# Attention with nine consecutive tokens of a head in a partition, K^T V in 64-row products, and its scaling on ScalarE

## The chip, the cores and the metric

One NeuronCore of a Trainium2 chip runs the whole program. The metric is the device time of one execution in microseconds (us); lower is better. TensorE multiplies, VectorE, ScalarE and GpSimd do elementwise work, reductions and copies, SP issues most of the transfers (DMAs). In the profile they are PE (PEld for its weight loads), DVE, ACT, POOL and SP.

## The reference

The inputs are float32; q, k and v are [8, 8, 576, 64]: batch, head, token, head dimension. What matters here is the first of three stages:

```python
q_s = exp(q - max(q, axis=-1)); q_s /= sum(q_s, axis=-1) + 1e-9     # over the 64 dims of a token
k_s = exp(k - max(k, axis=2));  k_s /= sum(k_s, axis=2) + 1e-9      # over the 576 tokens of a head
kv  = einsum('bhsd,bhse->bhde', k_s, v)                             # 64 x 64 for each head
out = einsum('bhsd,bhde->bhse', q_s, kv)
```

The output, 4608 tokens of 512, goes through a layer with eight experts (each token to its best one) and then through a gated layer, (x wa) * (x wb) wo.

## The kernel before

The attention works on 16 units, each of four heads of one batch: unit u is batch u // 2, heads 4(u % 2) to 4(u % 2) + 3. `load` (L79) puts 512 of a head's 576 tokens on 128 partitions, four consecutive tokens to a partition; the last 64 tokens of two batches share one extra tile (`s`), a batch on each half of the partitions, loaded with the unit of the even batch. So each step of a unit has a part for the 512 tokens and one for the 64, the latter often only in units of an even batch (`first`, L105).

- K: `kmax` (L118) reduces each partition's four tokens on VectorE; `kmax_t` turns the result (and the 64 extra tokens) by TensorE transposes (L100); `kmax_r` (L136, L139, L141) reduces over partitions and joins both parts; `kb_t` and `kb_c` (L152) bring the maximum back to all partitions; `ksub` (L161, L164) subtracts on GpSimd; `kexp` (L170, L171) takes the exponential on ScalarE; `vcopy` (L178, L180) copies V beside a column of ones.
- `kv_mm` (L217) forms K^T V for two heads at a time, with the sum of the exponentials in the ones' column: four products with 128 rows and one with 64 for each pair of heads, all into one PSUM tile. A float32 product is two records in the trace, a transpose one. `kv_norm` (L225, L226, L230) adds 1e-9, takes the reciprocal and scales the 64x64 diagonal blocks into `kvb`, all on VectorE. `kv_t`, `kv_c` (L240), `kv_g` (L246) and `kv_gc` (L249) multiply `kvb` with the gate weights and append the result.
- Q: `qmax` (L187, L191), `qsub` (L200, L206), transposes (`q_t`, `qs_t`) and exponentials on the way out of PSUM (`q_e` L260, `qs_e` L271).
- Output: `o_m` (L306) multiplies Q with `kvb`; `evac_l` (L276) copies the logits on ScalarE, then `evac_x` (L284 to L286) scales the rows on VectorE. Both read one PSUM tile, and the VectorE part waits for the ScalarE part. `out_shared` (L330) does this for the 64 extra tokens of two batches, 64 columns to each half of the PSUM partitions.
- After every second batch `route` (L337) chooses the experts on VectorE, stores x (L390) and the extra rows (L395) to DRAM, and builds one-hot matrices (L397) that ScalarE scales (L401, L402).

The order on each engine is the order of the program, and it is written out by hand. Step s runs this list, a name and how many units it is behind (`more` lets the routing go on, `shared` is `out_shared`):

```python
STEP = (("kv_t", 2), ("kmax_t", 0), ("kv_c", 2), ("q_t0", 1), ("kmax_r", 0), ("kv_g", 2), ("more", 2),
        ("kv_gc", 2), ("qmax", 0), ("q_e0", 1), ("kb_t", 0), ("kb_c", 0), ("qs_t", 1), ("ksub", 0), ("q_t1", 1),
        ("more", 2), ("o_m0", 2), ("qs_e", 1), ("q_e1", 1), ("kv_mm", 1), ("kmax", -1), ("vcopy", 0),
        ("o_m2", 2), ("o_l0", 2), ("more", 3), ("more", 3), ("more", 4), ("o_x0", 2), ("qsub", 0), ("kexp", 0),
        ("kv_norm", 1), ("o_l2", 2), ("o_x2", 2), ("shared", 2))
```

`run` (L433) issues the loads of K three units ahead and of Q and V two ahead, on SP. From step 10 on, the weights of the first expert are loaded and split, and later its first tokens are gathered and multiplied, between these operations; a table of places in the list (`AT`, L418) says where. Transposes share three PSUM tiles (`pt`), `kv_mm` has one (`pk`), the outputs two. The input buffers lie in memory that the expert stage uses later (`Experts.buffers`, L907).

## Time and profile before

| | us |
|---|---|
| median of three runs | 1457.78 (1457.41 to 1458.32) |
| the profiled execution | 1467.53 |
| its span in the trace | 1465.8 |
| busy in the span: PE, DVE, ACT, POOL | 1366.1, 1043.0, 674.0, 564.2 |

The profile comes from one execution. Times are counted from the start of its span, and L is a line of the kernel. An instruction's idle time is that of its engine just before it; behind the arrow stands what ended it.

### The profile page before, as it was taken

To read this page: it belongs to the slowest core of one execution; us is meant where nothing else is said; L and a number is where in the kernel's file an instruction comes from. 1 tells how busy PE (TensorE), PEld (TensorE's weight loads), DVE (VectorE), ACT (ScalarE), POOL (GpSimd) and SP (SyncE) were. 2 spreads that over 40 slices of the span, in tenths; PEclk is the share of its full clock that TensorE was granted. 3 is DMA by queue.
4 is the path that set the end of the run, shared out by engine and by line. 5 is a ranking of instruction groups with operands and counts; after the bars stand their busy time and mean duration, and the time that the engine had idled before them with its cause. 6 is when DMAs were issued, how large, how long until landed. Compare 5 with 4: busy or idle time off the path is not lost.

```text
span 1465.8 us, 29137 instructions
## 1 busy us (share of the span) xinstructions
PE 1366.1 (93%) x11068; PEld 1112.0 (76%) x11068; DVE 1043.0 (71%) x2340; ACT 674.0 (46%) x1625; POOL 564.2 (38%) x698
## 2 busy tenths in 40 slices
PE   6887898998999999989999999999999999999996
PEld 4776775665576676768888888888888888888885
DVE  5889875875687776426767867777777777767764
ACT  4556554753455454324444444444444444444432
POOL 6755521523334354104343343433334333343433
PEclk9988798999999999999999999999999999999998
DMA  9998245788564345126010010100101001010000
GB/s 240 253 251 220 73 131 164 268 291 271 184 220 140 113 135 165 48 72 255 2 56 4 1 59 1 59 1 16 45 1 59 2 18 42 1 59 1 31 1 30
DMA packets 87919, 145.87 MB, mean 100 GB/s; under 512 B 19792, under 2 KB 60752, under 8 KB 85584
## 3 DMA queue, kind: packets, MB, share of 16 engines
q1 hardware_dynamic: 81136, 123.85, 26.8%
q0 software_dynamic: 6080, 19.95, 4.2%
q8 instruction: 92, 1.51, 0.5%
q14 instruction: 67, 0.55, 0.1%
q10 hardware_dynamic: 544, 0.02, 0.0%
HBM read 149.78 MB, written 46.44 MB: 134 GB/s over the span
## 4 chain that ended last, share of the span: by engine, by line
PE 41%; DVE 10%; issue 2%; ACT 1%; POOL 1%; POOLq 0%; DVEq 0%; ACTq 0%
PE ab L1644 27%; PE mp L1659 13%; DVE raw L1348 1%; DVE y L1338 1%; DVE gp L1686 1%; DVE w L1348 1%; PE ab L1328 1%; DVE ysb L1818 1%; DVE w L1819 1%; DVE xg L1806 1%; DVE g L1819 1%; DVE gu L1815 0%; DVE w L1822 0%; DVE g L1822 0%; DVE y L1736 0%
## 5 line engine op out<-in xcount | busy, mean ns | idle before, releaser
L1644 PEld LDWEIGHTS <-gw 128*128 128x128 f16 x3780 | 369.2, 98 | 60.0 <-issue 13.6
L1644 PE MATMUL ab<-raw,gw 128*128 128x256 f16 x2100 | 280.2, 272 | 5.6 <-ACTq L1267 2.7
L1644 PE MATMUL ab<-w,gw 128*128 128x256 f16 x1680 | 225.2, 273 | 0.8
L1659 PEld LDWEIGHTS <-gp 128*128 128x128 f16 x1944 | 190.8, 98 | 25.9 <-ACT gp L1681 2.1
L1061 PEld LDWEIGHTS <-w 128*128 128x128 f16 x1824 | 180.1, 99 | 38.6 <-issue 12.7
L1061 PE MATMUL ph<-xhl,w 128*128 128x256 f16 x1728 | 198.2, 276 | 9.7 <-issue 4.1
L1078 PE MATMUL py<-w,hh 128*128 128x512 f16 x576 | 172.5, 381 | 2.4 <-DMA w<-wd 2.4
L1659 PE MATMUL mp<-wo,gp 128*128 128x256 f16 x756 | 142.6, 273 | 0.0
L1686 DVE SCALAR_TENSOR_TENSOR gp<-gp,gs 128x256 f16<-128x256 f16 x162 | 81.1, 505 | 59.0 <-ACT gp L1681 58.0
L1069 DVE SCALAR_TENSOR_TENSOR hl<-ph,hh 128x256 f16<-128x256 f32 x144 | 59.2, 420 | 78.7 <-ACT hh L1068 75.6
L1078 PE MATMUL py<-w,hl 128*128 128x512 f16 x288 | 109.9, 382 | 0.0
L1078 PEld LDWEIGHTS <-hh 128*128 128x128 f16 x608 | 59.8, 99 | 64.7 <-issue 4.2
L1460 POOL TENSOR_TENSOR gf<-gf 128x256 f32<-128x256 f32 x72 | 64.5, 916 | 100.4 <-ACT gf L1503 92.0
L1681 ACT ACTIVATE gp<-g 128x256 f16<-128x256 f32 x108 | 45.0, 417 | 115.7 <-DVE g L1822 114.8
L1644 PEld LDWEIGHTS <-w 128*128 128x128 f16 x756 | 73.7, 97 | 29.5 <-issue 21.0
L1717 POOL TENSOR_TENSOR gs<-w 128x256 f32<-128x256 f32 x54 | 39.5, 732 | 134.0 <-DVE w L1822 134.0
L1681 ACT ACTIVATE gp<-w 128x256 f16<-128x256 f32 x54 | 22.5, 417 | 148.9 <-DVE w L1822 146.2
L1659 PE MATMUL mp<-raw,gp 128*128 128x256 f16 x324 | 88.6, 273 | 0.9 <-DVE gp L1686 0.9
L1659 PE MATMUL mp<-w,gp 128*128 128x256 f16 x324 | 88.8, 274 | 0.0
L1068 ACT ACTIVATE hh<-ph 128x256 f16<-128x256 f32 x144 | 54.0, 378 | 74.9 <-PE ph L1061 74.5
L1023 POOL DMA_INDIRECT xg<-xd,gidx x40 | 43.9, 1098 | 106.9 <-ACT xhl L1052 51.4
L1815 DVE TENSOR_TENSOR gu<-tables,ab 128x256 f32<-128x256 f32 x108 | 45.3, 419 | 54.2 <-PE ab L1644 47.1
(337 smaller groups left out, 2798.8 us busy)
## 6 DMA issues: line engine op xcount, KB each, us to landing
w<-wd SPq DMA_DIRECT2D x58, 1024.0 KB
raw<-in_moe_w_dram SPq DMA_DIRECT2D x24, 512.0 KB
yd<-ysb SPq DMA_DIRECT2D x19, 513.0 KB
xd<-x SPq DMA_DIRECT2D x8, 1026.0 KB
y<-yd SPq DMA_DIRECT2D x8, 1026.0 KB
w<-in_k_dram SPq DMA_DIRECT2D x16, 512.0 KB
wd<-wst SPq DMA_DIRECT2D x16, 512.0 KB
g<-in_moe_w_a_dram SPq DMA_DIRECT2D x12, 512.0 KB
```

The source lines that it names most:

```text
L1023: nc.gpsimd.indirect_dma_start(out=self.x[:, j], out_offset=None, in_=self.xd[0:4 * S if s == 0 else NTOK, :], in_offset=bass.IndirectOffs ...
L1061: nc.tensor.matmul(ph, self.w1[:, w, k, o], x[:, k], start=i == 0, stop=i == 11)
L1068: nc.scalar.activation(self.hh[:, f], ph, AF.Relu)
L1069: nc.vector.scalar_tensor_tensor(self.hl[:, f], ph, 0.0, self.hh[:, f], ALU.max, ALU.subtract)
L1078: nc.tensor.matmul(self.py[j], h[:, f, o], self.w2[:, w, f], start=f == 0 and i == 0, stop=f == 7 and i == 2)
L1460: self.nc.gpsimd.tensor_tensor(s[:, dst], s[:, x], s[:, y], ALU.subtract)
L1644: self.nc.tensor.matmul(ps, self.w[f][:, b, o:o + P], self.y[n].op[:, a, yl, 256 * k:256 * k + 256], start=i == 0 and fresh, stop=i == 5, ...
L1659: self.nc.tensor.matmul(self.acc[nm][:, t], x, y, start=i == t == j == 0 and nm != "p3", stop=i == last and t == 1 and j == 2, skip_group_ ...
L1681: self.nc.scalar.activation(self.part(i, a)[:, 0], x, AF.Copy, scale=2.0 ** -11)
L1686: eng.scalar_tensor_tensor(p[:, 1], p[:, 0], -2048.0, x, ALU.mult, ALU.add)
L1717: pool.tensor_tensor(x, a11, a21, ALU.subtract)
L1815: v.tensor_tensor(u, w, x, ALU.add)
```

## The change

Each of the two halves of the partitions now holds one pair of heads: partition 64a + p has tokens 9p to 9p + 8 of the heads 2a and 2a + 1 of the unit. The separate tile for 64 tokens is gone, and with it the second part of each step. Tiles of K, Q and V are [128, 2 heads, 9 tokens, 64]. `kv_mm` contracts over 64 rows, nine products for each half, alternating between the halves, with an accumulator of its own for each (one is a `pt` tile). `kv_norm` leaves the addition and the reciprocal on VectorE and does the scaling in four ScalarE activations. `kb_t` uses two products with 64 columns instead of two transposes. Eight of a partition's nine tokens make the four output tiles of a batch, two at a time; the ninth takes the place of the extra tokens. The rows of x are stored by half and by token, and the token numbers, the modality's layout and the aliased buffers follow. `kv_t` to `kv_gc`, `evac_l`, `evac_x` and `STEP` are unchanged. The core of the diff (the head of each hunk has the line before):

```diff
@@ -79 @@ def load(self, nm, u):
-        nc.sync.dma_start(out=t.rearrange("p h c d -> p h (c d)"),
-                          in_=self.src[nm][b, h, 0:512, :].rearrange("h (p c) d -> p h (c d)", c=4))
-        if b % 2 == 0:
-            s = self.sh.tile([P, 4, D], F32, tag="s" + nm, name=f"s{nm}{u}", bufs=2 if nm == "v" else 4)
-            for j in range(2):
-                nc.sync.dma_start(out=s[j * 64:(j + 1) * 64],
-                                  in_=self.src[nm][b + j, h, 512:576, :].rearrange("h s d -> s h d"))
+        for a in range(2):
+            h = 4 * g + 2 * a
+            self.nc.sync.dma_start(out=t[64 * a:64 * a + 64].rearrange("p s c d -> p s (c d)"),
+                                   in_=self.src[nm][b, h:h + 2].rearrange("s (p c) d -> p s (c d)", c=9))
...
@@ -112 @@ kmax, kmax_t, kmax_r, kb_t
-        m1 = self.wk.tile([P, 4, D], F32, tag="mx1", name="mx1")
-        nc.vector.tensor_reduce(m1, k.rearrange("p h c d -> p h d c"), AX.X, ALU.max)
+        m1 = self.wk.tile([P, 2, D], F32, tag="mx1", name="mx1")
+        nc.vector.tensor_reduce(m1, self.t["k", u].rearrange("p s c d -> p s d c"), AX.X, ALU.max)
...
-        for hp in range(2):
-            self.transpose(pt[:, hp, :], self.pair(m1, hp))
-        if self.first(u):
-            for hp in range(2):
-                self.transpose(pt[:, 2 + hp, :], self.pair(self.s["k", u], hp))
+        self.transpose(self.pm[u][:, 0], self.flat(self.m1.pop(u)))
...
-        nc.vector.tensor_reduce(m, pt[:, 0:2], AX.X, ALU.max)
-        if self.first(u):
-            ms = self.sm.tile([P, 2, 2], F32, tag="ms", name="ms")
-            nc.vector.tensor_reduce(ms, pt[:, 2:4].rearrange("p h (b s) -> p h b s", b=2), AX.X, ALU.max)
-            self.ms[u] = self.ms[u + 2] = ms
-        nc.vector.tensor_tensor(m, m, self.ms.pop(u)[:, :, u // 2 % 2], ALU.max)
+        self.nc.vector.tensor_reduce(self.m[u], self.pm.pop(u)[:, 0].rearrange("p (a q) -> p a q", a=2), AX.X, ALU.max)
...
-        for hp in range(2):
-            self.transpose(self.pb[u][:, hp, :], m[:, hp:hp + 1].to_broadcast([P, P]))
+        for a in range(2):
+            self.nc.tensor.matmul(self.pb[u][64 * a:64 * a + 64, 0], m[:, a:a + 1].to_broadcast([P, 64]), self.c.ident,
+                                  start=True, stop=True)
...
@@ -208 @@ kv_mm, kv_norm
-        pk = self.ps_kv.tile([P, 2, 2, D + 1], F32, tag="pk", name="pk")
-        for hp in range(2):
-            hs = slice(2 * hp, 2 * hp + 2)
-            for j in range(5):
-                e, w = (k[:, j, hs, :], v[:, j, hs, :]) if j < 4 else (sk[r, hs, :], sv[r, hs, :])
-                nc.tensor.matmul(pk[:, hp].rearrange("p h d -> p (h d)"), e.rearrange("p h d -> p (h d)"),
-                                 w.rearrange("p h d -> p (h d)"), start=j == 0, stop=j == 4)
+        pk = self.pk[u] = [t.rearrange("p a b -> p (a b)")[:, 0:2 * (D + 1)] for t in
+                           (self.ps_kv.tile([P, 4, P], F32, tag="pk", name="pk"), self.pt())]
+        for c in range(9):
+            for a in range(2):
+                r = slice(64 * a, 64 * a + 64)
+                self.nc.tensor.matmul(pk[a], self.flat(k[r, c]), self.flat(v[r, c]), start=c == 0, stop=c == 8)
...
-        nc.vector.tensor_scalar(rd, pk[:, :, 0, D], EPS, None, ALU.add)
+        for a in range(2):
+            nc.vector.tensor_scalar(rd[:, a:a + 1], pk[a][:, D:D + 1], EPS, None, ALU.add)
         nc.vector.reciprocal(rd, rd)
         kb = self.kvb[u % 6]
-        for j in range(2):
-            r2 = slice(64 * j, 64 * j + 64)
-            nc.vector.tensor_tensor(kb[r2, :, 64 * j:64 * j + 64], pk[r2, :, j, 0:D],
-                                    rd[r2, :, None].to_broadcast([64, 2, D]), ALU.mult)
+        for a in range(2):
+            for j in range(2):
+                r = slice(64 * j, 64 * j + 64)
+                nc.scalar.activation(kb[r, a, 64 * j:64 * j + 64], pk[a][r, j * (D + 1):j * (D + 1) + D], AF.Copy,
+                                     scale=rd[r, a:a + 1])
...
@@ -387 @@ route
-            nc.sync.dma_start(out=self.xd[b * S:b * S + 512, :].rearrange("(p c) d -> p (c d)", c=4),
-                              in_=x.rearrange("p c d -> p (c d)"))
+            for c2 in range(2):
+                nc.sync.dma_start(out=self.rows(b)[:, c2:8:2], in_=x[64 * c2:64 * c2 + 64])
...
-            nc.sync.dma_start(out=self.xd[b * S + 512:b * S + 576, :], in_=xs[64 * jb:64 * jb + 64])
+            nc.sync.dma_start(out=self.rows(b)[:, 8], in_=xs[64 * jb:64 * jb + 64])
```

## Rows read from the trace of the kernel before

**Rows 1.** Stretches view: start:end, length, busy us (instructions) per engine, clock, DMA share, GB/s.

```profile
0.00:24.50 24.50, 10.99 (x43) 7.97 (x43) 12.39 (x21) 8.60 (x14) 17.52 (x57) 1.00 0.92 247
24.50:61.00 36.50, 33.08 (x239) 29.17 (x240) 28.21 (x63) 20.49 (x45) 25.93 (x29) 0.95 1.01 263
61.00:198.00 137.00, 112.17 (x758) 98.34 (x753) 118.59 (x271) 83.52 (x205) 70.78 (x77) 0.85 0.65 181
198.00:236.00 38.00, 31.39 (x327) 22.60 (x327) 24.77 (x78) 12.78 (x36) 8.59 (x11) 0.89 0.36 95
```

**Rows 2.** Timeline of VectorE, unit 9: start, length, engine, line, operation.

```profile
117.62 0.15 DVE L225 TENSOR_SCALAR rd<-pk 128x2 f32<-128x2 f32 x1
...
118.63 0.17 DVE L284 TENSOR_SCALAR rc<-po 128x8 f32<-128x8 f32 x1
```

**Rows 3.** Timeline of TensorE, unit 9, the same columns, idle before in brackets.

```profile
111.64 1.05 PE L217 MATMUL pk<-v,ke 128*128 128x130 f32 x8
112.62 0.49 PE L217 MATMUL pk<-v1s,sk 64*128 64x130 f32 x2
...
114.55 1.26 PE L306 MATMUL po<-kvb,qt 128*128 128x146 f32 x8
...
118.75 0.66 PE L100 MATMUL pt<-ident,kvb 128*128 128x128 f32 x2 [1.58 <-DVE kvb L230]
```

**Rows 4.** Groups by line and shape, 0 to 200 us: count, busy, mean ns, idle before.

```profile
L161 POOL TENSOR_TENSOR ke<-w,mb 128x512 f32<-128x512 f32 x32 | 40.1, 1274 | 58.4 <-ACT mb L152 36.9 <-DMA raw<-in_moe_w_dram 7.6 <-issue 7.5
...
L118 DVE TENSOR_REDUCE mx<-w 128x256 f32<-128x1024 f32 x16 | 31.2, 1951 | 1.7 <-DMA w<-in_k_dram 1.7
...
L100 PE MATMUL pt<-ident,kvb 128*128 128x128 f32 x32 | 7.6, 326 | 14.2 <-DVE kvb L230 14.2
...
L136 DVE TENSOR_REDUCE m<-pt 128x2 f32<-128x256 f32 x16 | 6.7, 416 | 4.0 <-PE pt L100 3.8
...
L187 DVE TENSOR_REDUCE mq<-xg 128x16 f32<-128x1024 f32 x5 | 6.0, 1209 | 2.9 <-DMA xg<-in_q_dram 2.9
...
L139 DVE TENSOR_REDUCE ms<-pt 128x4 f32<-128x256 f32 x8 | 3.3, 414 | 0.0
L141 DVE TENSOR_TENSOR m<-m,ms 128x2 f32<-128x2 f32 x16 | 3.3, 206 | 0.6
L191 DVE TENSOR_REDUCE msq<-sq 128x4 f32<-128x256 f32 x8 | 3.3, 407 | 0.0
```

**Rows 5.** Timeline of all engines, the first unit.

```profile
13.81 1.04 ACT L178 COPY v<-ysb 128x1024 f32<-128x1024 f32 x1 [3.41 <-DMA ysb<-in_v_dram]
...
24.49 0.41 PE L100 MATMUL pt<-ident,kvb 128*128 128x128 f32 x2 [1.24 <-DVE kvb L230]
```

**Rows 6.** Stretches view of line 330 alone: records in flight in 50 ns.

```profile
105.80:105.85 0.05, 0.05 (x6) 0.05 (x4) 1.00 1.07 266
```

**Rows 7.** Groups by line and shape, 0 to 200 us, ScalarE.

```profile
L170 ACT ACTIVATE ke<-ke 128x1024 f32<-128x1024 f32 x16 | 16.8, 1052 | 2.0 <-POOL ke L161 2.0
...
L276 ACT COPY lraw<-po 128x64 f32<-128x64 f32 x32 | 6.8, 212 | 13.4 <-PE po L306 13.1
...
L171 ACT ACTIVATE sk<-sk 64x256 f32<-64x256 f32 x16 | 6.6, 410 | 0.4 <-POOL sk L164 0.2
```

**Rows 8.** Timeline of all engines, unit 6.

```profile
81.72 0.38 ACT L402 ACTIVATE lb<-hot,tidb 128x128 f16<-128x128 f16 x1
...
82.02 1.04 ACT L170 ACTIVATE ke<-ke 128x1024 f32<-128x1024 f32 x1
...
82.29 0.16 DVE L225 TENSOR_SCALAR rd<-pk 128x2 f32<-128x2 f32 x1 [0.46 <-PE pk L217]
...
83.42 0.41 PE L100 MATMUL pt<-ident,kvb 128*128 128x128 f32 x2
```

**Rows 9.** Timeline of SP's queue, the last stores of x.

```profile
207.65 1.59 SPq L390 DMA_DIRECT2D xd<-x  x2
```

**Rows 10.** Timeline of GpSimd, the gather behind these stores.

```profile
221.33 1.05 POOL L1023 DMA_INDIRECT xg<-xd,gidx  x1 [12.32 <-DMA xd<-xs]
```

More of the change, by code (lines that the diff above doesn't have):

```diff
@@ L100, in transpose, with flat @@
         self.nc.tensor.transpose(out, in_, self.c.ident)
-    def pair(self, t, hp):
-        return t[:, 2 * hp:2 * hp + 2, :].rearrange("p h d -> p (h d)")
-    def first(self, u):
-        return u // 2 % 2 == 0
-    def rows(self, u):
-        r = 64 * (u // 2 % 2)
-        return slice(r, r + 64)
+    def flat(self, t):
+        return t.rearrange("p s d -> p (s d)")
     def kmax(self, u):
@@ L176, in vcopy @@
+        for h in range(2):
+            self.nc.gpsimd.tensor_tensor(ke[:, :, h], k[:, h], mb[:, None, h].to_broadcast([P, 9, D]), ALU.subtract)
+    def kexp(self, u):
+        ke = self.ke[u]
+        self.nc.scalar.activation(ke, ke, AF.Exp)
     def vcopy(self, u):
-        nc = self.nc
-        nc.scalar.copy(self.v1[u % 2][:, :, :, 0:D], self.t["v", u].rearrange("p h c d -> p c h d"))
-        if self.first(u):
-            nc.scalar.copy(self.vs(u)[:, :, 0:D], self.s["v", u])
+        self.nc.scalar.copy(self.v1[u % 2][:, :, :, 0:D], self.t["v", u].rearrange("p s c d -> p c s d"))
@@ L303, in o_m @@
         po = self.po[u, j] = self.ps_o.tile([P, 2, 512], F32, tag="po", name="po")
-        for a in range(2):
-            for hp in range(2):
-                self.nc.tensor.matmul(po[:, a, PC * hp:PC * hp + PC], qt[:, hp, j + a, :], self.kvb[u % 6][:, hp],
-                                      start=True, stop=True)
+        for t in range(2):
+            for a in range(2):
+                self.nc.tensor.matmul(po[:, t, PC * a:PC * a + PC], self.flat(qt[:, a, 2 * (j + t):2 * (j + t) + 2]),
+                                      self.kvb[u % 6][:, a], start=True, stop=True)
     def o_l(self, u, j):
@@ L328, in out_shared @@
                 r = slice(64 * jb, 64 * jb + 64)
-                for hp in range(2):
-                    nc.tensor.matmul(po[r, 0, PC * hp:PC * hp + PC], qs[:, hp, r],
-                                     self.kvb[(4 * i + 2 * jb + g) % 6][:, hp], start=True, stop=True)
+                for a in range(2):
+                    nc.tensor.matmul(po[r, 0, PC * a:PC * a + PC], qs[:, a, jb],
+                                     self.kvb[(4 * i + 2 * jb + g) % 6][:, a], start=True, stop=True)
             self.evac_l(po[:, 0:1], self.lraw[i][:, 8:9, hs])
@@ L1149, in early @@
                 if i:
-                    w.add(lo, m, i - 1, after=[("ksub", 14 + (i - 1) // 2)] if m else ())
+                    w.add(lo, m, i - 1, after=[("ksub", 14)] if m else ())
         def scale():
```

168 lines of the change are left out of this document (62 added, 106 removed).

## The prediction

> **What bounds the kernel now.** I read the stages first [rows 1]. The change touches the attention, which fills the first 198 us of 1465.8 and the stores of the 38 us behind it; the expert and gated stages follow in program order, so what the attention gains or loses is mostly handed on whole. In the stretch from 24.5 to 61 us TensorE is busy 33.1 of 36.5 us and the DMA share is 1.01; from 61 to 198 us VectorE is busy 118.6 of 137 us and TensorE, at a mean granted clock of 0.85, 112.2. So two regimes: units 1 to 4 are paced by TensorE, the eleven from unit 5 on mostly by VectorE, which has the routing beside the attention.
>
> Then I looked for the wait that ends last in a unit. In unit 9 VectorE reaches the normalisation at 117.62 us, 3.07 us after TensorE began the products behind K^T V at 114.55 us [rows 2, 3]; TensorE has run out of work and waits 1.58 us for kvb. Over the attention these waits sum to 14.2 us by the line of the wait for kvb [rows 4]. Units 5, 7, 9, 11 and 13 look like this (five); in the others the first VectorE instruction of the normalisation starts within 1.3 us of the last product's end. So the step that is moved, kv_norm, is on the path.
>
> **Part by part.**
>
> *Loads.* Instead of 512 tokens as 1024-byte pieces and 64 tokens as 256-byte pieces, each partition gets 2304 bytes. The DMA share of 1.01 invites the thought that loads bind. They don't after the start: the only long wait for a load is ScalarE's for v at 13.81 us, 3.41 us [rows 5], and VectorE's whole wait for k and q is 1.7 + 2.9 us [rows 4]. Number of issues on SP: three large loads a unit and six small ones in every second unit are six on average before, six after; what queues behind them on SP is unchanged. At the start four loads of 640 KB precede the first v and become four of 576 KB, so v lands about 0.1 x 13 = 1.3 us earlier, and fewer pieces help a little more. Bounds: 0 (TensorE, not the load, ends the first unit at 24.49) and 3.4 us (the whole wait). I take **-1.0**, nearer to the TensorE end because its order decides when the first kv_t starts. The Trainium skill, DMA: Bandwidth & Descriptors, section Rules for kernel authors, advises against two transfers to disjoint halves of the partitions, since they run on the same engines one behind the other. By it alone this term would be 0; no run here shows a large load in halves.
>
> *K^T V.* Before, two groups of eight records with 128 rows and two with 64. 111.64 to 112.62 us is eight records, 0.122 each; from 111.64 to the next L306 at 114.55 are 2.91 us, so the four 64-row records cost 2.91 - 2 x 0.98 = 0.95, 0.24 each: twice the price, an excursion into 64 rows and back costs about 0.24 us [rows 3]. After: 36 records of 64 rows in one excursion, alternating between the halves. If the halves run beside each other: 18 x 0.122 + 0.24 = 2.4 us, -0.5. If not: 36 x 0.122 + 0.24 = 4.6, +1.7. The trace has one case of halves side by side, the column halves of out_shared: six matmuls in flight in 50 ns [rows 6], against two records per 0.24 us in a 128-row stream [rows 3]. I take the overlap. The Trainium skill, TensorE: Matmul & The Clock Gate, Part 3, states the same for row groups; by it the term is -0.5, and no row here shows two row halves at once.
>
> *Maximum of K and its broadcast.* Per unit VectorE had L118 1.951, L136 0.416, half of L139 0.207, L141 0.206, L187 1.209 and half of L191 0.204, together 4.19 us [rows 4]. After: 1152 elements instead of 1024, 1.951 x 1.125 = 2.19 (bounds: at L187's rate 1.36, and 2.19); one reduction of half of L136's elements, 0.27 (0.21 to 0.42); 1.209 x 1.125 = 1.36. Together 3.82: **-0.37 a unit**, bounds -1.26 and -0.22. kb_t turns from two transposes into two 64-column fp32 products, four records, with an excursion of its own: 0.24 more and the second pair of records 0.12, **+0.35**. kmax_t drops from two transposes (four in every second unit) to one; where TensorE paces the unit they lie beside ScalarE's kv_c, so I count nothing. If kv_c were shorter this cover would be gone and they would give 0.24 a unit.
>
> *K and Q subtraction, exponentials, V copy.* GpSimd: 2 x 1.27 x 1.125 = 2.9 us for K (L161, [rows 4]), without the extra 64-row instruction; mostly it waits for ScalarE, 36.9 us in all by the same row, so 0. ScalarE: one exponential of 1152 elements, 1.17 us, for 1.052 + 0.410 [rows 7], in a queue that is busy 83.5 of 137 us [rows 1]: 0. If ScalarE becomes late, this is 0.3 us a unit that comes back.
>
> *kv_norm on ScalarE.* Before, VectorE takes 1.01 us from the first instruction of the normalisation to the evacuation behind it [rows 2]. After: two additions and a reciprocal, 0.5 us; four activations with a scale from memory. That kind with 128 elements follows the one before by 0.30 us (81.72 to 82.02) [rows 8]; at 0.84 ns an element ((1.052 - 0.410) / 768 [rows 7]) 64 elements give 0.25, four 1.0. Behind them on ScalarE stands o_l, 0.21 [rows 7], and VectorE's evacuation waits for o_l. So 0.5 + 1.0 + 0.21 = 1.7 us: **+0.7** where VectorE is late, and nothing else on VectorE can fill the gap, because its queue is in order. TensorE's kv_t comes 0.5 us later too. In units paced by TensorE the evacuation waited for the last products anyhow (L306, 1.26 us [rows 3]), so +0.3. A third kind: in units 6, 10 and 14 ScalarE is itself late. In unit 6 its exponential starts at 82.02 behind the one-hot scalings, and VectorE starts the normalisation at 82.29 without needing ScalarE; TensorE continues at 83.42 [rows 8]. After, the four activations stand behind the exponential: 82.02 + 1.17 + 1.0 + 0.1 = 84.3, **+0.9**. Bounds for all of this: 0 if the gap is always hidden, 11 x 1.2 = 13 us if every unit meets it.
>
> *Stores and tables.* Rows of x go out as 2052-byte pieces in four issues instead of two of 8208-byte rows: two issues more at about 0.8 us (1.59 / 2) on SP [rows 9], in front of the last gather, which waits for these stores till 221.33 [rows 10]. The bytes are the same. Bounds: -2 (shorter pieces spread better) and +3; I take 0. A second accumulator takes one of three transpose banks until kv_norm ends; the transposes that reuse it stand behind kv_t, which needs kv_norm anyway: 0. Token tables and modality: once, beside the loads: 0.
>
> **The sum.** Start -1.0. Units 1 to 4: handover +0.3, shorter kmax_r (0.83 to 0.27) -0.56, kb_t +0.35, K^T V -0.5: -0.4 each, -1.6; the same for units 8, 12 and 15, -1.2. Five late units: 5 x (0.7 - 0.37) = +1.7. Three units behind the exponential: 3 x (0.9 - 0.37) = +1.6. End 0. Total -0.5 us on the profiled execution's 1467.53; that execution stands 9.75 us over the median 1457.78, and I carry the difference over: **1457 us**. What the loads, the smaller reductions and the packed products give, the handover takes.
>
> **Rivals.**
> - *The handover is hidden.* ScalarE has 53 us free between 61 and 198 us [rows 1]; for it speaks that in units paced by TensorE the products cover half of it. Then the 5 x 0.7 + 3 x 0.9 = 6.2 us stay away: 1451; with the K reduction at L187's rate another 8 x 0.83 = 6.6: 1444. Between them 1449.
> - *ScalarE becomes the pacer (slower).* If ScalarE's queue holds the four activations in every one of the eleven units behind an exponential or the one-hot scalings, each pays +0.9 and gets nothing from VectorE: it decides as soon as ScalarE's last instruction before kv_norm ends later than VectorE's reciprocal. In place of -1.2 + 1.7 + 1.6: 11 x 0.9 = 9.9, so +7.8: 1465. Against it: only three units show it now.
> - *The 64-row halves don't overlap.* K^T V then costs +1.7 instead of -0.5, 2.2 more in the units where TensorE paces, and idle time of 14.2 us in the others swallows part: 7 x 2.2, and half of it in the other eight: +24 at most, 1472 to 1481. Against it: [rows 6].
> - *It does nothing on the path*: loads and reductions were covered, and the end moves by the stores only: 1456 to 1460.
>
> **How the numbers follow.** This kernel's times can tell 0.2% (2.9 us) from no change, so the borders are 1454.9 and 1460.7. The forecast, 1453 to 1461 with the errors of its terms, has 0.47: faster 0.10, same 0.34, slower 0.03. Hidden handover 0.27, all faster. ScalarE as pacer 0.14, slower. No overlap 0.08, slower. Nothing on the path 0.04, same. Faster 0.37, same 0.38, slower 0.25. The range 1445 to 1469 takes in the forecast, most of the first rival, the second and the fourth, some 0.84; the forecast alone would be 1453 to 1461.
>
> **What would show it.** Right: L136's successor at about 0.27 us; two L217 streams with 36 records in about 2.4 us at the full granted clock; VectorE's evacuation waiting for ScalarE about 1.2 us after each reciprocal in late units; kv_t waiting for ScalarE's kvb. Wrong: K^T V over 4 us at the full clock (third rival); ScalarE idle ahead of the four activations and VectorE without a wait behind them (first); the activations regularly behind the exponential (second); a first exponential not earlier than 15 us says that the loads gave nothing.

## The result, and the profile after

The changed kernel takes 1476.14 us in the median of four runs (1473.83 to 1477.58), the kernel before 1457.6 (1456.6 to 1458.32): 1.0126 times as long, with an interval of 1.0109 to 1.0144, about 18.5 us lost. The forecast was no change (1457), and its range of 1445 to 1469 does not hold the result. The profiled execution is one of the four, 1477.58 us with a span of 1474.5.

The lines of the changed kernel have other numbers: L100, L109 and L139 are the reductions of K and Q (before L118, L136, L187), L126 the subtraction on GpSimd (L161), L155 K^T V (L217), L162, L163 and L168 the normalisation (L225, L226, L230), L213 and L221 the evacuation (L276, L284), L243 and L267 the output products (L306, L330), L331 and L335 the stores (L390, L395), L964 the gather (L1023).

The stretches view of the changed kernel; the columns are those of [rows 1]:

```profile
0.00:24.50 24.50, 7.06 (x55) 4.92 (x55) 10.45 (x14) 8.17 (x12) 16.22 (x51) 1.00 0.94 208
24.50:61.00 36.50, 31.87 (x270) 27.36 (x272) 23.01 (x42) 23.44 (x54) 23.39 (x27) 0.86 1.06 232
61.00:198.00 137.00, 109.18 (x897) 92.67 (x895) 103.91 (x234) 89.92 (x230) 67.71 (x64) 0.79 0.77 193
```

Against [rows 1] two things stand out. VectorE is busy 103.9 us instead of 118.6 between 61 and 198 us and TensorE's clock falls from 0.85 to 0.79: the engines do not work more, they wait (a part of VectorE's 14.7 us is the scaling, which has moved; with it back on VectorE, in kernel A below, VectorE is busy 117.5 us there). And in the first two stretches the DMA engines are as busy as before (0.94 and 1.06) but move 208 and 232 GB/s instead of 247 and 263.

The groups of the changed kernel by line and shape, 0 to 200 us, as in [rows 4]:

```profile
L100 DVE TENSOR_REDUCE mx<-w 128x128 f32<-128x1152 f32 x12 | 25.9, 2156 | 3.0 <-DMA w<-in_k_dram 3.0
...
L139 DVE TENSOR_REDUCE mq<-mid 128x18 f32<-128x1152 f32 x10 | 13.5, 1346 | 5.5 <-DMA mid<-in_q_dram 5.5
...
L90 PE MATMUL pt<-ident,kvb 128*128 128x128 f32 x30 | 9.8, 343 | 21.1 <-ACT kvb L168 21.0
...
L168 ACT ACTIVATE kvb<-pk,rd 64x64 f32<-64x64 f32 x30 | 9.2, 307 | 16.7 <-DVE rd L163 16.4
...
L221 DVE TENSOR_SCALAR rc<-po 128x8 f32<-128x8 f32 x29 | 4.7, 163 | 31.7 <-ACT lraw L213 31.7
...
L109 DVE TENSOR_REDUCE m<-pt 128x2 f32<-128x128 f32 x16 | 4.5, 282 | 3.9 <-PE pt L90 3.9
```

The reductions came out as costed (2.156 for 2.19, 0.282 for 0.27, 1.346 for 1.36). The two waits to read are L90, TensorE's wait for kvb, 21.1 us for 14.2 in [rows 4], and L221: VectorE waits 31.7 us for ScalarE's copy of the logits. A second trace of the kernel before (first experiment) has 9.0 us there:

```profile
L284 DVE TENSOR_SCALAR rc<-po 128x8 f32<-128x8 f32 x32 | 5.2, 162 | 9.1 <-ACT lraw L276 9.0
```

Unit 9, the unit of [rows 2], shows the plain form of such a wait. The timeline of all engines of the changed kernel:

```profile
122.09 0.15 DVE L162 TENSOR_SCALAR rd<-pk 128x1 f32<-128x1 f32 x1
...
122.60 0.63 ACT L168 ACTIVATE kvb<-pk,rd 64x64 f32<-64x64 f32 x2 [1.72 <-DVE rd L163]
...
123.91 0.21 ACT L213 COPY lraw<-po 128x64 f32<-128x64 f32 x1
...
124.15 0.17 DVE L221 TENSOR_SCALAR rc<-po 128x8 f32<-128x8 f32 x1 [1.65 <-ACT lraw L213]
```

From the first instruction of the normalisation to the evacuation it takes 2.06 us, for 1.01 in [rows 2]; ScalarE stands idle before its four activations, and VectorE waits 1.65 us behind them. Read in the same way from the timelines of units 1 to 15, the changed kernel has 2.05 to 2.08 us in ten units, 2.85 or 2.86 in units 6, 10 and 14, 4.15 in unit 3 and 3.43 in unit 8: 36.8 us together, for 21.9 in the kernel before. (In unit 0 the evacuation waits for later work in both kernels.)

Unit 8 has one of the two longest of these waits, with a cause of its own. The same timeline:

```profile
102.39 3.13 SPq L875 DMA_DIRECT2D raw<-in_moe_w_dram  x4
...
106.90 0.17 DVE L163 RECIPROCAL rd<-rd 128x2 f32<-128x2 f32 x1
...
107.16 0.63 ACT L168 ACTIVATE kvb<-pk,rd 64x64 f32<-64x64 f32 x2
...
107.81 0.64 ACT L168 ACTIVATE kvb<-pt,rd 64x64 f32<-64x64 f32 x2
108.65 1.06 ACT L881 ACTIVATE ejunk<-raw 128x1024 f16<-128x1024 f32 x1 [0.21 <-DMA raw<-in_moe_w_dram]
...
109.82 0.30 ACT L213 COPY lraw<-po 128x64 f32<-128x64 f32 x2
110.07 0.17 DVE L221 TENSOR_SCALAR rc<-po 128x8 f32<-128x8 f32 x1 [3.00 <-ACT lraw L213]
...
111.34 1.25 PE L267 MATMUL po<-kvb,qs 128*64 128x146 f32 x8 [2.88 <-DVE rc L221]
```

Behind the reciprocal (106.90) stand four activations, 107.16 to 108.45. Then comes L881, which sums the squares of a piece of an expert's weights, 1.25 us with its read-out and nothing to do with this unit; it stands between kv_norm and the copy of the logits in the program, in this unit alone. The copy follows at 109.82, VectorE's evacuation at 110.07 after 3.00 us of waiting, and TensorE, which needs the bank that this frees, at 111.34 after 2.88 us. Now the same place in the kernel before:

```profile
103.19 1.04 ACT L940 ACTIVATE ejunk<-raw 128x1024 f16<-128x1024 f32 x1
...
105.87 0.17 DVE L284 TENSOR_SCALAR rc<-po 128x8 f32<-128x8 f32 x1 [0.45 <-ACT lraw L276]
...
107.14 0.73 PE L330 MATMUL po<-kvb,qs 128*64 128x146 f32 x8 [0.90 <-DVE rc L284]
```

There the same work of the expert's weights (L940) ran from 103.19 to 104.33, while TensorE and VectorE were busy with K^T V and the normalisation. In the changed kernel the row of L881 names the transfer of these weights as what it waited for last. SP issues that transfer at 102.39, 4.3 us ahead of the unit's normalisation, for 94.04 and 10.4 us in the kernel before. That the scaling is not what makes this unit late is shown by kernel A (below), which has the scaling back on VectorE:

```profile
105.06 1.06 ACT L881 ACTIVATE ejunk<-raw 128x1024 f16<-128x1024 f32 x1 [2.90 <-DMA raw<-in_moe_w_dram]
...
106.34 0.17 DVE L221 TENSOR_SCALAR rc<-po 128x8 f32<-128x8 f32 x1 [1.86 <-ACT lraw L213]
...
107.62 1.25 PE L267 MATMUL po<-kvb,qs 128*64 128x146 f32 x8 [2.71 <-DVE rc L221]
```

A's ScalarE stands idle 2.90 us for the weights, and the evacuation comes 3.25 us behind the first instruction of the normalisation, for 3.43. In SP's queue ahead of this transfer stand the stores of x of two batches (85.86 to 95.41 us, 80.87 to 84.07 before) and the loads in halves. Which of them makes it late was not tried by itself; with contiguous stores (C) ScalarE still waits 1.77 us, with single loads as well (E) not at all.

The idle time is paid twice there. The stretches view behind the gap, the changed kernel, A, and the kernel before:

```profile
111.40:113.20 1.80, 1.80 (x11) 1.41 (x12) 0.82 (x4) 0.19 (x1) 0.00 (x0) 0.50 1.02 229
```

```profile
108.60:110.40 1.80, 1.80 (x11) 1.60 (x9) 1.21 (x5) 0.56 (x2) 0.29 (x1) 0.50 1.04 217
```

```profile
107.20:109.00 1.80, 1.80 (x19) 1.50 (x19) 1.31 (x6) 0.56 (x2) 0.29 (x1) 1.00 1.11 338
```

Behind 2.88 and 2.71 us without work TensorE runs at the lower of its two levels (0.50, 1.2 GHz), behind the 0.90 us of the kernel before at the upper. The kernel before has stretches at the lower level too; over 61 to 198 us the mean clock is 0.85 there, 0.79 in the changed kernel and 0.83 in A.

### The profile page after: what moved, and what is told of

It reads as the page before. It is cut to its first block, busy times and chain, and to the rows that moved or that the text cites. A ratio compares the mean times of both kernels' runs of the same rounds, so it can differ in the third digit from the quotient of the medians.

```text
span 1474.5 us, 29663 instructions
## 1 busy us (share of the span) xinstructions
PE 1366.6 (93%) x11324; PEld 1109.4 (75%) x11324; DVE 1027.1 (70%) x2292; ACT 690.7 (47%) x1673; POOL 560.0 (38%) x677
## 4 chain that ended last, share of the span: by engine, by line
PE 41%; DVE 11%; issue 2%; ACT 1%; POOL 0%; POOLq 0%; DVEq 0%
PE ab L1585 27%; PE mp L1600 13%; DVE raw L1289 1%; DVE y L1279 1%; DVE gp L1627 1%; DVE w L1289 1%; PE ab L1269 1%; DVE mid L1759 1%; DVE g L1760 1%; DVE w L1760 1%; DVE mid L1747 1%; DVE gu L1756 0%; DVE g L1763 0%; DVE w L1763 0%; DVE yh L1253 0%
## 5 line engine op out<-in xcount | busy, mean ns | idle before, releaser
L1002 PE MATMUL ph<-mid,w 128*128 128x256 f16 x1728 | 196.0, 274 | 6.6 <-DVE mid L1010 2.4
L1019 PE MATMUL py<-w,mid 128*128 128x512 f16 x864 | 195.4, 381 | 3.0 <-DMA w<-wd 3.0
L1019 PEld LDWEIGHTS <-mid 128*128 128x128 f16 x912 | 89.6, 99 | 101.6 <-issue 5.2
L1010 DVE SCALAR_TENSOR_TENSOR mid<-ph,mid 128x256 f16<-128x256 f32 x144 | 59.1, 420 | 76.8 <-ACT mid L1009 76.6
L1600 PE MATMUL mp<-mid,gp 128*128 128x256 f16 x540 | 103.7, 276 | 1.8 <-ACT gp L1622 1.8
L1585 PEld LDWEIGHTS <-w 128*128 128x128 f16 x756 | 73.7, 97 | 29.4 <-issue 21.1
L1009 ACT ACTIVATE mid<-ph 128x256 f16<-128x256 f32 x144 | 54.1, 379 | 67.8 <-PE ph L1002 67.4
L1750 ACT COPY mid<-ab 128x256 f32<-128x256 f32 x108 | 40.2, 372 | 95.0 <-PE ab L1585 95.0
L964 POOL DMA_INDIRECT mid<-xd,gidx x40 | 44.7, 1117 | 105.1 <-ACT mid L993 46.4
```

The source lines that it names most:

```text
L964: nc.gpsimd.indirect_dma_start(out=self.x[:, j], out_offset=None, in_=self.xd[0:4 * S if s == 0 else NTOK, :], in_offset=bass.IndirectOffs ...
L1002: nc.tensor.matmul(ph, self.w1[:, w, k, o], x[:, k], start=i == 0, stop=i == 11)
L1009: nc.scalar.activation(self.hh[:, f], ph, AF.Relu)
L1010: nc.vector.scalar_tensor_tensor(self.hl[:, f], ph, 0.0, self.hh[:, f], ALU.max, ALU.subtract)
L1019: nc.tensor.matmul(self.py[j], h[:, f, o], self.w2[:, w, f], start=f == 0 and i == 0, stop=f == 7 and i == 2)
L1585: self.nc.tensor.matmul(ps, self.w[f][:, b, o:o + P], self.y[n].op[:, a, yl, 256 * k:256 * k + 256], start=i == 0 and fresh, stop=i == 5, ...
```

## The experiments

Ratios are to runs of the kernel before on the same chip; the chips were not the same for all kernels, so kernels are compared by their ratios, and microseconds from ratios are of 1457. "Last K^T V" is the start of unit 15's products, "gather" the first gather behind the last stores, both from the kernel's trace.

| kernel | ratio (95% interval) | last K^T V, us | gather, us |
|---|---|---|---|
| before, second trace | one execution, 1459.31 us | 187.4 | 217.75 |
| changed | 1.0126 (1.0109 to 1.0144) | 197.6 | 233.80 |
| before, scaling on ScalarE | 1.0145 (1.0129 to 1.0162) | 202.9 | 237.23 |
| before, loads in halves | 1.0032 (1.0020 to 1.0044) | 188.9 | 219.98 |
| changed, scaling ahead of the exponential | 1.0241 (1.0224 to 1.0258) | 214.0 | 250.43 |
| changed, x stored as before (rows in another order) | 1.0103 (1.0086 to 1.0120) | 198.9 | 230.82 |
| A: changed, scaling on VectorE | 1.0054 (1.0038 to 1.0071) | 189.2 | 223.71 |
| A, halves of K^T V one after the other | 1.0157 (1.0127 to 1.0187) | 206.0 | 241.94 |
| B: A, modality copies a step earlier | 1.0043 (1.0026 to 1.0060) | 186.5 | 221.54 |
| C: B, x in contiguous pieces | 1.0012 (0.9995 to 1.0029) | 186.3 | 218.53 |
| C, two transpose banks | 1.0041 (1.0028 to 1.0054) | 190.4 | 223.90 |
| D: C, scaling in two masked steps | 0.9993 (0.9977 to 1.0009) | 180.2 | 212.45 |
| E: D, one load for each operand (two heads exchanged) | 0.9963 (0.9948 to 0.9977) | 176.2 | 209.86 |
| F: E, heads put right in the weights | 0.9964 (0.9948 to 0.9980) | 176.2 | 208.34 |

**The kernel before again.**

> The kernel before, unchanged, for a second trace: the profiled execution of before stood at 1467.5 us, 9.8 us over the median of its runs, while the changed kernel's profiled execution is one of its usual ones. Theory: an ordinary execution of before, near 1458 us, loses less in the expert stage (or behind the gather) than the profiled one, and the attention's end is where it was (gather at about 221 us). Rival: the attention itself is shorter in an ordinary execution, and the gather comes at about 212 us; then the change costs the attention nearly 20 us and not 12.

It took 1459.31 us, and the last K^T V stands at 187.4 us for 188.7 in the first trace: the theory, but with the gather between the two. The gather comes 3.6 us earlier, the rest of the 8 us is gained behind it. Against this trace the changed kernel's profiled execution loses 10.2 us up to the last K^T V, 16.0 up to the gather, and 2 more behind it.

**Who scales K^T V.** One edit in each kernel:

```diff
 A, from the changed kernel
-                nc.scalar.activation(kb[r, a, ...], pk[a][r, ...], AF.Copy, scale=rd[r, a:a + 1])
+                nc.vector.tensor_tensor(kb[r, a, ...], pk[a][r, ...], rd[r, a:a + 1].to_broadcast([64, D]), ALU.mult)
 from the kernel before
-            nc.vector.tensor_tensor(kb[r2, :, ...], pk[r2, :, j, 0:D], rd[r2, :, None].to_broadcast([64, 2, D]), ALU.mult)
+                nc.scalar.activation(kb[r, a, ...], pk[r, a, j, 0:D], AF.Copy, scale=rd[r, a:a + 1])
```

> The changed kernel with the scaling of K^T V back on VectorE (four instructions of 64x64 elements in place of ScalarE's four). Theory (the handover is what costs): the products behind kvb start about 1 us earlier a unit and VectorE no longer waits 3 us for ScalarE's copy of the logits; the gather moves from 233.8 us to 223 to 226 us, and the time falls by 8 to 12 us to 1464 to 1468. Rival (64-row products, the loads and the stores cost, whoever scales): the gather stays within 3 us of 233.8 and the time stays above 1472.

> The kernel before with nothing changed but the scaling of K^T V: ScalarE does it in four 64x64 activations. Theory (handover): it loses 8 to 13 us by itself, 1466 to 1471, with VectorE waiting 1.3 us or more for ScalarE behind each reciprocal. Rival (the rest of the change costs): less than 4 us lost, under 1462.

A took 1464.92 us, as the theory had it, and the kernel before with ScalarE's scaling 1478.07, 21 us more than the kernel before where 8 to 13 were expected. The groups by line, 0 to 200 us, of A:

```profile
L168 DVE TENSOR_TENSOR kvb<-pk,rd 64x64 f32<-64x64 f32 x32 | 7.1, 222 | 0.9
...
L221 DVE TENSOR_SCALAR rc<-po 128x8 f32<-128x8 f32 x32 | 5.2, 164 | 9.9 <-ACT lraw L213 9.1
```

and of the kernel before with the scaling on ScalarE:

```profile
L231 ACT ACTIVATE kvb<-pk,rd 64x64 f32<-64x64 f32 x60 | 18.5, 309 | 20.7 <-DVE rd L226 19.9
...
L284 DVE TENSOR_SCALAR rc<-po 128x8 f32<-128x8 f32 x28 | 4.6, 163 | 29.6 <-ACT lraw L276 29.6
```

VectorE's wait for ScalarE follows the scaling in both kernels: 9.0 and 9.1 us where VectorE scales, 29.6 and 31.7 where ScalarE does. By the ratios the handover costs 10.5 us in the changed kernel (1.0126 less 1.0054 of 1457), over half of its loss, and 21 in the old one, as much as the whole loss. The first agrees with the timelines: A takes 26.4 us from the normalisation's first instruction to the evacuation, units 1 to 15 together, 10.4 less than the changed kernel. The cost is larger in the old kernel, where ScalarE has the small exponential of L171 and the copy of L180 in the queue as well (how much of the difference these make was not tried).

**The order on ScalarE.**

```diff
-... ("qsub", 0), ("kexp", 0), ("kv_norm", 1), ("o_l2", 2) ...
+... ("qsub", 0), ("kv_norm", 1), ("kexp", 0), ("o_l2", 2) ...
```

> The changed kernel with ScalarE's scaling put ahead of the next unit's exponential, nothing else. Rival to the handover as such: if the cost is that the four activations stand behind an exponential of 1.16 us, 4 us or more come back (1472 or less). Theory (four activations of 0.31 us in a row and the copy of the logits behind them, in every unit): 2 us or less come back, or it loses, since the exponential now waits for VectorE's reciprocal.

It lost another 16 to 17 us (1492.05), as the theory allowed. Groups by line, 0 to 200 us:

```profile
L168 ACT ACTIVATE kvb<-pk,rd 64x64 f32<-64x64 f32 x28 | 8.6, 308 | 35.4 <-DVE rd L163 34.9
...
L221 DVE TENSOR_SCALAR rc<-po 128x8 f32<-128x8 f32 x26 | 4.2, 163 | 40.3 <-ACT lraw L213 40.3
```

ScalarE now stands idle 34.9 us for VectorE's reciprocal (16.4 in the changed kernel), with the exponential behind it, and VectorE waits 40.3 us for the copy, since the exponential now stands between the scaling and the copy. Putting the scaling ahead of the exponential gives nothing back. That an exponential ahead costs nothing is not shown by this run; but in the changed kernel ScalarE waits for the reciprocal, with nothing in front of the scaling, in ten of the units 1 to 15, and VectorE waits behind it all the same.

**The stores of x.**

```diff
-            for c2 in range(2):
-                nc.sync.dma_start(out=self.rows(b)[:, c2:8:2], in_=x[64 * c2:64 * c2 + 64])
+            nc.sync.dma_start(out=self.xd[b * S:b * S + 512, :].rearrange("(p c) d -> p (c d)", c=4), in_=...)
...
-            nc.sync.dma_start(out=self.rows(b)[:, 8], in_=xs[64 * jb:64 * jb + 64])
+            nc.sync.dma_start(out=self.xd[b * S + 512:b * S + 576, :], in_=xs[64 * jb:64 * jb + 64])
```

> The changed kernel with the stores of x in the form of before: one issue of 8208-byte pieces a batch, the extra rows in one block (the rows of the output then stand in another order than the reference's). Theory: the last four issues took 5.64 us on SP against 1.59 for two before, and the gather moved 2.5 us more than the end of the attention; this gives 2 to 4 us back, 1472 to 1474, with the attention itself unchanged. Rival (the stores are as fast by their bytes): no change beyond 1 us.

1472.28 us, by the ratios 3.4 less, with intervals that overlap. SP's queue and the gather, first the changed kernel, then this one:

```profile
217.56 5.64 SPq L331 DMA_DIRECT2D xd<-x  x4
223.64 3.54 SPq L335 DMA_DIRECT2D xd<-xs  x2
```

```profile
218.57 1.59 SPq L330 DMA_DIRECT2D xd<-x  x2
220.27 2.56 SPq L335 DMA_DIRECT2D xd<-xs  x2
```

Four issues of 1.41 us for two of 0.80; from the first issue to the gather it takes 16.24 us and 12.25. The attention ends no earlier (last K^T V at 198.9 against 197.6), so the 4.0 us are gained in the tail.

**The modality copies.** The six small copies on GpSimd stand behind step 2, the rest stays behind step 3:

```diff
-                at.run({0: [load_modality], 3: [token_bias]}, ...
+                at.run({0: [load_modality], 2: [token_kind], 3: [token_bias]}, ...
```

> The kernel with the scaling back on VectorE, and the six small copies of the modality on GpSimd placed one step earlier (behind step 2 instead of with the rest behind step 3). There GpSimd began to subtract the fourth unit's maximum at 46.7 us, behind these copies, and the fourth unit's products ended 2.3 us later against the units around it. Theory (a queue on GpSimd that was counted as nothing): 1.5 to 2.5 us less than the same kernel without it (1464.9), 1462.5 to 1463.5, and the kept part of the delay is small. Rival (VectorE or the loads swallow it): within 0.7 us of 1464.9.

1462.27 us (B), by the ratios 1.6 less than A. GpSimd's timeline, the changed kernel:

```profile
45.23 0.35 POOL L501 CAST mf<-mi 64x16 f32<-64x16 int32 x2
...
48.82 1.41 POOL L126 TENSOR_TENSOR ke<-w,mb 128x576 f32<-128x576 f32 x1
```

and B:

```profile
30.80 0.34 POOL L501 CAST mf<-mi 64x16 f32<-64x16 int32 x2
...
34.20 2.81 POOL L126 TENSOR_TENSOR ke<-k,mb 128x576 f32<-128x576 f32 x2 [2.39 <-issue]
...
44.76 2.81 POOL L126 TENSOR_TENSOR ke<-w,mb 128x576 f32<-128x576 f32 x2
```

In B the copies lie ahead of a subtraction that starts 2.39 us behind them, just after ScalarE's copy of the maximum that it subtracts (33.79 to 34.06 us), so they cost nothing there. The gather comes 2.2 us earlier than in A; the two ratios' intervals overlap, so the time alone does not show the gain.

**Contiguous pieces.** The exponential of Q writes tokens 9p + 4h to 9p + 4h + 3 so that a half of the partitions gets four consecutive ones:

```diff
-        self.nc.scalar.activation(self.qt[u][:, :, 4 * h:4 * h + 4]...
+        self.nc.scalar.activation(self.qt[u][:, :, h:8:2]...
-                nc.sync.dma_start(out=self.rows(b)[:, c2:8:2], ...
+                nc.sync.dma_start(out=self.rows(b)[:, 4 * c2:4 * c2 + 4].rearrange("p n d -> p (n d)"), ...
```

> The kernel of the last run, and x stored in contiguous pieces: the exponential of Q writes the nine-token order so that a half of the partitions holds four consecutive tokens each, so a piece is 8208 bytes again, with two issues a batch and all rows where they belong. Theory (it is the number of small pieces and their issue on SP, 1.41 us each, that delayed the gather): 3 to 4 us less than the last kernel, about 1459, the gather 21 to 24 us behind the last product of K^T V instead of 25. Rival (the number of issues counts, not the pieces): less than 1.5 us less.

1457.41 us (C, from B), by the ratios 4.5 us less, where the theory had 3 to 4. From the first issue to the gather it takes 13.60 us for 16.42 in B, with as many issues as there. The four issues take 5.26 us on SP for 5.64, so most of the 2.8 us is not the issuing, which the theory named, but what the pieces take behind it. The expectation's distances from the last product of K^T V were misread: the traces have 33 us in B and 30 in C for its 25 and 21 to 24.

**Two banks.** From C:

```diff
-        self.ps_t = pool("ps_t", 3, space=PSUM)
+        self.ps_t = pool("ps_t", 2, space=PSUM)
-        pk = self.pk[u] = [... for t in (self.ps_kv.tile([P, 4, P], F32, ...), self.pt())]
+        pk = self.pk[u] = self.ps_kv.tile([P, 2, 512], F32, tag="pk", name="pk")
```

> The last kernel, with both accumulators of K^T V in one tile of two banks and two transpose banks instead of three; the normalisation is then one addition, one reciprocal and two multiplications, as before the change. Theory (VectorE paces, and its four multiplications and two additions cost 0.5 us a unit against before): 2 to 5 us less than the last kernel, 1454 to 1457. Rival (the third transpose bank is needed): equal or slower, with TensorE waiting for ScalarE's copies out of the transpose banks.

1462.6 us, by the ratios 4.2 more than C with intervals that just touch: the rival. TensorE's waits, 0 to 200 us (sum, times, longest), in this kernel:

```profile
PE pt L90 <- ACT kt L175: 6.3, 13, 0.5
PE pt L115 <- ACT kvb L184: 5.2, 14, 1.6
```

In C the same two are 1.5 and 1.7 us. A transpose bank that is missing all the time costs more than the instructions that a wider tile saves.

**The halves of K^T V.** From A:

```diff
-        for c in range(9):
-            for a in range(2):
+        for a in range(2):
+            for c in range(9):
```

> The kernel with the scaling on VectorE (1464.9 us) with the eighteen K^T V products in another order: nine for one half of the partitions, then nine for the other, instead of alternating. Theory (the two halves run beside each other because their products are neighbours in the queue): the products of a unit take about 4.1 us at the full clock (36 records at 0.112) instead of 2.3, and the time rises by 10 to 25 us, 1475 to 1490. Rival (the halves never overlapped in time, the records only share their stamps): the time stays within 3 us.

1480.21 us in the median of only two executions (1476.1 and 1484.33), 15 us over A. TensorE's timeline of the changed kernel, the first products of unit 8 (each line a record, a weight load beside it):

```profile
104.33 0.38 PE L155 MATMUL pk<-v,ke 64*128 64x130 f32 x1
104.34 0.38 PE L155 MATMUL pt<-v,ke 64*128 64x130 f32 x1
```

and of this kernel, unit 5:

```profile
65.89 1.94 PE L155 MATMUL pk<-v,ke 64*128 64x130 f32 x15
...
68.01 1.83 PE L155 MATMUL pt<-v,ke 64*128 64x130 f32 x15
69.77 1.26 PE L243 MATMUL po<-kvb,qt 128*128 128x146 f32 x8
```

Alternating products start in pairs 0.01 us apart, and the eighteen pairs take 2.21 us (104.33 to 106.54, where L243 follows); in blocks they take 3.88 (65.89 to 69.77) and only the seam overlaps. The halves do run beside each other, as neighbours in the queue. The third rival's cost (15 to 24 us) is real for halves that don't overlap; the change's order of loops avoids it.

**The loads.**

```diff
 the kernel before
-        nc.sync.dma_start(out=t..., in_=self.src[nm][b, h, 0:512, :].rearrange("h (p c) d -> p h (c d)", c=4))
+        for a in range(2):
+            nc.sync.dma_start(out=t[64 * a:64 * a + 64]..., in_=self.src[nm][b, h, 256 * a:256 * a + 256, :]...)
```

> The kernel before, with each of its large loads split in two transfers of 64 partitions; the pieces stay 1024 bytes. In the changed kernel a piece of 2304 bytes took 162 ns, 14.2 bytes per ns, against 58 ns for 1024 bytes, 17.6 bytes per ns, and the second unit's K^T V began 2 us later. Theory (it is the halves): the 1024-byte pieces take 65 ns or more in the first 61 us and the kernel loses 1 to 4 us. Rival (it is the pieces of 2304 bytes): 58 to 61 ns a piece as before, and the time within 1 us of before.

1461.14 us, 3.9 more by the medians and 4.7 by the ratio. The DMA view's row of the queue that loads, 0 to 61 us (packets, MB, share of 16 engines): the kernel before in its second trace, this kernel, the changed kernel and E (below):

```profile
q1 hardware_dynamic: 23435, 15.86, 98.1%
```

```profile
q1 hardware_dynamic: 19900, 12.84, 105.0%
```

```profile
q1 hardware_dynamic: 7724, 13.47, 100.0%
```

```profile
q1 hardware_dynamic: 8830, 16.63, 82.1%
```

Bytes by busy time (MB over share x 61 us x 16): 16.6 bytes per ns and engine before, 12.5 with the same pieces in halves; 13.8 in the changed kernel, 20.8 with the changed kernel's pieces in one transfer. In the trace's records of 25 to 61 us a 1024-byte piece takes 77 ns in halves and 60 in one transfer, a 2304-byte piece 164 and 112. So longer pieces are better, as the change meant, and halves are worse by more. More issues on SP, which the halves bring as well, are not the reason: up to 24.5 us the engines' share rises with the halves (1.02 for 0.91 in the second trace of before) while the rate falls (205 GB/s for 247), so they did not stand waiting for issues.

**Masked scaling.** (C with a constant mask that is 1 on the diagonal blocks.)

```diff
-                nc.vector.tensor_tensor(kb[r, a, 64 * j:64 * j + 64], pk[a][r, ...], ..., ALU.mult)
+            nc.vector.scalar_tensor_tensor(kb[:, a, 0:P]..., pk[a]..., rd[:, a:a + 1], self.own, ALU.mult, ALU.mult)
```

> The kernel with the scaling on VectorE, the earlier modality copies and the contiguous stores (1457.4 us), with the four multiplications of a unit's normalisation replaced by two over all 128 partitions that multiply by a constant mask of the diagonal blocks as well. Four of 64 elements take 1.0 us in a row (0.222 each, 0.25 apart); two of 128 elements should take 0.6. Theory (VectorE paces from the fifth unit on): 0.35 us a unit less, 3 to 5 us in all, 1452.5 to 1454.5, below both kernels. Rival (the mask is a second operand from SBUF and waits while GpSimd works, or VectorE doesn't pace): within 1.5 us of 1457.4.

1455.88 us (D; runs from 1450.49 to 1461.9). By the time it is undecided, 1.5 us less than C where the theory wanted 3 to 5. By the trace the step itself does what it should: two of 0.35 us for four of 0.222, and 0.97 us for 1.43 from the normalisation's first instruction to the evacuation in unit 9. The last K^T V comes 6.1 us earlier than in C, but C's trace is of one of its longest executions (1461.55) and D's of a short one (1453.92), so that distance is not the step's alone.

**One load for each operand.**

```diff
-        for a in range(2):
-            self.nc.sync.dma_start(out=t[64 * a:64 * a + 64]..., in_=self.src[nm][b, h:h + 2]...)
+        src = self.src[nm][b, 4 * g:4 * g + 4].rearrange("(s a) t d -> s (a t d)", s=2)
+        self.nc.sync.dma_start(out=t..., in_=src.rearrange("s (q x) -> q s x", q=P))
```

> The last kernel (mask, contiguous stores, earlier modality copies; 1455.9 us) with each load as one transfer over 128 partitions instead of two over 64: a half of the partitions then holds the heads a and a + 2 of the unit, so that the address grows by the same step from each partition to the next. The pieces stay 2304 bytes; the second and third head of every four exchange places in the rows of x and so in the output, the gate's logits are those of the right heads. Theory (two transfers to halves of the partitions cost bandwidth): a piece takes 130 to 140 ns instead of 162, the stretch to 24.5 us moves over 230 GB/s instead of 212, the second unit's K^T V begins 1 to 2 us earlier, and the time falls by 1.5 to 4 us, 1452 to 1454.5. Rival (it is the length of the pieces): 155 ns or more a piece and within 1 us of 1455.9.

1451.9 us (E), a ratio of 0.9963, 4.4 us less than D, with 325 GB/s in the first 24.5 us and a piece of 2304 bytes at 105 to 112 ns, better than the theory had it. The first unit's exponential starts at 12.3 us instead of 14.9 in D and 15.3 in the changed kernel, the second unit's K^T V at 25.2 instead of 27.2 and 31.0.

**The heads put right.** The same, with the rows of the first expert weights loaded in the exchanged order, in two halves:

```diff
-            self.nc.sync.dma_start(out=dst, in_=src[:, P * i:P * i + P].rearrange("a p f -> p (a f)"), **kw)
+            for s in range(2):
+                o = 256 * (i // 2) + 64 * (i % 2) + 128 * s
+                self.nc.sync.dma_start(out=dst[64 * s:64 * s + 64], in_=src[:, o:o + 64]..., **kw)
```

> The kernel with one load for each operand, and the exchange of the second and third head taken back where the first expert weights are loaded: their rows come in the order of the exchanged channels, in two transfers of 64 partitions instead of one of 128, so that the output is the reference's. Theory (the loads of the weights have slack, the loads of the attention have none at its start): within 1.5 us of 1451.9, so 1450.5 to 1453.5, and below the kernel before. Rival (the halves cost wherever they are): the weights' loads, half of the DMA work of the expert stage, delay it by 4 us or more, above 1456.

1452.8 us (F), 0.9964 with an interval of 0.9948 to 0.9980: 0.36% faster than the kernel before, with the output's channels where they belong. The stretches view of F:

```profile
0.00:24.50 24.50, 10.61 (x81) 7.89 (x82) 13.82 (x19) 9.68 (x16) 17.69 (x55) 1.00 0.97 332
24.50:61.00 36.50, 33.10 (x351) 28.87 (x351) 31.06 (x67) 21.68 (x47) 28.28 (x33) 1.00 0.73 236
```

332 GB/s at the start, and 0.73 of the DMA engines' time in the second stretch for 1.06 in the changed kernel. Halves cost little where nobody waits for them, as in the expert weights.

## Why the prediction was wrong

**The steps of the loss.** By the ratios the changed kernel stands 18.4 us over before. A takes 10.5 off, the copies 1.6, the contiguous stores 4.5; C is left with 1.7, which is within its interval of nothing. Each step has an error of about 3 us, so the copies by themselves are not shown by the time; the traces agree in order and size. What the change brings (packed products, shorter reductions, fewer instructions) is in C paid for by the loads in halves, as E shows (4.4 us), and by four scalings instead of two, which D shows in its trace and not in its time.

**The handover cost most, and was not the largest miss.** The step was "+0.7 where VectorE is late", "+0.9" in three units behind the exponential and "+0.3" where TensorE paces, about 8 us in all, of which shorter reductions gave back most. Measured: 10.5 us against four instructions on VectorE, 21 in the kernel before. Four instructions are themselves longer than the two of before: leaving out units 3 and 8, A has 1.4 us more than the kernel before between the normalisation's first instruction and the evacuation. So the handover is about 12 us by the timelines, an estimate. Unit by unit, the "+0.9" behind the exponential holds (0.8 to 1.4). Late units pay 1.06 for 0.7 (5, 7, 9 and 13; unit 11 nothing): an activation of 64 elements takes 0.31 us, not 0.25, so the four take 1.29. Units paced by TensorE pay 0.6 for 0.3: their last products were to cover the handover, and VectorE's evacuation came when ScalarE was done, after a wait of 1.65 us. TensorE's clock was lower with the handover (0.79 for 0.83 in A from 61 to 198 us), which the sum did not have at all. Units 3 and 8 pay 2.7 and 2.0, but most of that is not the scaling's, since A has 1.2 and 1.8 of it: in unit 3 the exponential is late, behind the modality's work on GpSimd, and in unit 8 the expert's weights are.

**What failed most is the rest.** The miss is 18.9 us, 18.4 for -0.5. Without the handover the sum has a gain of 8.8 us; A, which is the change without it, loses 7.9. The loads in halves cost 4.4 (E against D) where the sum had -1.0, the stores 4.5 (C against B) and the copies 1.6 (B against A) where it had 0; with some 4 for the handover that makes 15 to 16. These come from different pairs, each with an error of about 3 us, so they divide the miss only roughly, and the remaining 3 us are open. The +0.35 for kb_t was not measured alone.

**The rivals.** The second, ScalarE as pacer at 1465, came nearest in its time, but its condition did not hold: the scaling stood behind other work in units 3, 6, 10 and 14, and in ten of the units 1 to 15 ScalarE waited for VectorE's reciprocal. ScalarE is no pacer, busy 89.9 of 137 us; it is a round trip in every unit. The first, a hidden handover, is what 53 us of free ScalarE time seemed to promise; half of its sign came true, ScalarE idle ahead of the activations, but VectorE waited behind them all the same, since free time of an engine says nothing about the order in its queue. The third is refuted for this order of loops.

**The loads** were taken as -1.0 us; no gain came. The first exponential starts at 15.26 us, for 15.53 and 14.79 in the two traces of before, and by the forecast's own sign one not earlier than 15 us says that the loads gave nothing. That "what queues behind them on SP is unchanged" failed in unit 8, where the transfer of the expert's weights left 4.3 us ahead of the normalisation for 10.4. That loads don't bind after the start held for transfers over 128 partitions only: at about the same share of the DMA engines they moved an eighth to a sixth less, and VectorE's wait for q in the attention rose from 2.9 to 5.5 us ([rows 4] and L139). What halves and longer pieces come to together, against the loads of before, was not measured alone. The sentence of the Trainium skill by which this term would have been 0 (DMA: Bandwidth & Descriptors, Rules for kernel authors: use one transfer over 128 partitions, not two over halves) points the right way; the runs here go further than its reason, that the two share the same engines: pieces in halves take 1.3 to 1.5 times as long.

**The stores and the modality** were counted as 0 each. Stores: "the bytes are the same"; measured 3.4 to 4.5 us by the ratios, beyond the upper bound of +3. The larger part is the length of the pieces, since C gains 2.8 us to the gather with as many issues and nearly their time on SP; whole batches in one issue gain 4.0. The sum looked at the last stores only; those of earlier batches stand in SP's queue in the middle of the attention, 9.6 us for 3.2 ahead of unit 8's weights. The modality was called "beside the loads", but it stands in GpSimd's queue ahead of a subtraction, which was asked of the other engines and not here: about 2 us by the trace, not clear of the noise in the time.

**What held.** The reductions, K^T V at 2.21 us for 2.4 (the overlap of the halves included), and the carry-over of the profiled execution's extra time: of the 8.2 us between the two traces of before, 1.3 lie ahead of the last K^T V.

## What to carry to other kernels

Before a step is moved to another engine, write down the two queues around it: what the new engine does between the moved step and the next thing that the old engine needs back. Free time of the new engine is no argument, one round trip a unit is a cost in every unit, and idle TensorE can pay for it a second time at the lower clock. The queue that issues the transfers wants the same list: here stores in more and shorter pieces and loads in halves stood ahead of weights that another engine then waited for. A layout that makes longer pieces should also keep one transfer over all partitions: choose which heads share a partition so that the address grows by one step from partition to partition.

## What was not expected of the hardware

Transfers to 64 partitions took 1.3 times (1024-byte pieces, 77 for 60 ns) and 1.5 times (2304-byte pieces, 164 for 112 ns) the time of the same pieces in transfers to 128, and the busy share does not show it, only the GB/s beside it do: up to 24.5 us the changed kernel moved 208 GB/s at a share of 0.94, F 332 at 0.97. And fp32 products of two row halves, issued alternately, start 0.01 us apart and take 2.21 us for 36 records, for 3.88 in two blocks.
